# A spectral and token-mixing block, forward and backward on one core: the backward spectral part folded a second time, and its inverse rows interleaved with the weight gradients

## The chip, the core and the metric

One core of a Trainium2 chip. The metric is the device time of one execution, in microseconds; 367.74 us is the median of three runs of the kernel before (366.51 to 368.8). Engines: PE is TensorE, PEld its weight loads, DVE is VectorE, ACT is ScalarE, POOL is GpSimd, SP is SyncE, which issues most of the loads.

## What is computed

The input x has S = 2048 rows and D = 448 columns, bfloat16; F = 1792. Forward:

```python
h   = x + irfft2(rfft2(layernorm(x)) * (w_r + 1j * w_i))   # over rows and columns, 225 half-spectrum columns
u   = gelu(layernorm(h).T @ w1 + b1)                        # 448 x 1792: mixes the 2048 rows
out = h + (u @ w2 + b2).T
```

Outputs are out and the gradients with respect to x, w_r, w_i, w1, b1, w2 and b2 for a given grad_out (out_0 to out_7 in this order). The gradient of the spectral part is again a two-dimensional transform of a 2048 x 448 array (dh), a product with the conjugated weights, and an inverse transform.

## The kernel before

The rows are kept as 16 tiles (h) of 128 partitions. A two-dimensional transform has four steps, all by matrix multiplication with tables:

- fft_rows: for four tiles at a time, VectorE folds the 448 columns into sums and differences of column d and column 448 - d (even and odd part, 225 and 223 columns; L334 to L336), then four 128-wide matmuls a tile (L342) do a 16-point transform, evacuated into zt or zt2.
- fft_cols: for each r of 0 to 8 and its partner 16 - r, eight matmuls 225 columns wide with the table df (L361 to L375), two by two accumulated, then a copy by ScalarE (gi, L378), a sum and a difference by VectorE (gg, L381), three matmuls with hf (L353 to L355) and a copy (L356).
- cmul: the product with the spectral weights on VectorE, in six groups of rows r (L396 to L399); then ifft_cols: 256-wide matmuls (L413, L414) whose weights are 128 columns of the product w_b, and VectorE's sums into ab (L432, L434).
- ifft_rows: for each tile, four 225-wide matmuls with the table di (L443, L445), a ScalarE copy eo of 450 columns, and four matmuls with kinv (L449 to L452).

The program runs: forward spectral part; du = grad through w2 (L472); GELU; out (L627); dh (L683: 14 matmuls 449 columns wide a tile, whose last column is the row's sum of the bias gradient and gives the mean, then norm_back); the backward spectral part; weight gradients gw2 (14 blocks) and gw1 (16 blocks) by outer (L206, L213), each block 16 matmuls and four PSUM banks, copied out by ev (L225 on ScalarE, L226 on VectorE) and stored by POOL. norm_back is ScalarE's v (L650 or L652), then VectorE's L655, L657 and L658. grad_w, the gradient of w_r and w_i, is another cmul, of ds with xs_b, which is loaded again into the slot that goT held.

The order of instructions on each engine is fixed when the program is built: a list scheduler takes ready instructions in the order of the text, by its own estimate of times, and puts later ones that are ready into a wait. issue_after ties one instruction behind another on its engine. Every engine's queue then runs in that order. Tiles come from rings: ps_mm and ps_sp are four PSUM banks each; e4, k1, f2 and w4 have 3, 10, 3 and 4 buffers.

In the text before, the rows of the backward inverse come ahead of gw2 1 to 13, which come ahead of gw1; the scheduler has drawn gw2 and gw1 into the backward spectral part from 235 us on.

Of the kernel before, what the change touches and what calls it, by code (L numbers as in the profile page):

```python
# [11 lines left out]
BF16 = mybir.dt.bfloat16  # L12
# [5 lines left out]
P = 128  # L18
# [23 lines left out]
def _tables():  # L42
# [37 lines left out]
    tb["df1"] = _bf(dtab(wt))  # L80
    tb["df0"] = _bf(dtab(np.ones(DF)))

# [16 lines left out]
    wc[0] = 0  # L99
    tb["di1"] = _bf(itab(wc))  # L100
    pp = np.arange(P)
# [16 lines left out]
def kernel(  # L118
# [211 lines left out]

    def fft_rows(src, zt, g, on, behind=None):
        eo = e4([P, 4, D], "eo")
        a, b = src[:, 4 * g:4 * g + 4, 1:224], src[:, 4 * g:4 * g + 4, 447:224:-1]
        ve.tensor_tensor(out=eo[:, :, 1:224], in0=a, in1=b, op=ALU.add)  # L334
        ve.tensor_tensor(out=eo[:, :, 225:448], in0=a, in1=b, op=ALU.subtract)
        ve.tensor_copy(out=eo[:, :, 0:225:224], in_=src[:, 4 * g:4 * g + 4, 0:225:224])  # L336
        for i in range(4):
            h = 4 * g + i
            pz = ps_sp([P, 4, P])
            with tc.issue_after(behind.ins) if behind is not None else nullcontext():  # L340
                for c, o in enumerate((0, 97, 225, 320)):
                    last = pe.matmul(pz[:, c, :], lhsT=eo[:, i, o:o + P], rhs=kf[:], start=True, stop=True)  # L342
# [3 lines left out]
    def fft_cols(zt, dtab, dst, second=None):  # L346
        e_t = dtab[:, 0:2 * DF].rearrange("p (c k) -> p c k", c=2)
        o_t = dtab[:, 2 * DF:6 * DF].rearrange("p (c s k) -> p c s k", c=2, s=2)

        def out_r(r, gg):  # L350
            px = ps_sp([P, 2 * DF])
            k, i = R_ORDER.index(r) // 8, R_ORDER.index(r) % 8
            pe.matmul(px[:, :], lhsT=hf[:, k, 0, i, :], rhs=gg[:, :], start=True, stop=False)  # L353
            pe.matmul(px[:, 0:DF], lhsT=hf[:, k, 1, i, :], rhs=gg[:, DF:2 * DF], start=False, stop=False)
            pe.matmul(px[:, DF:2 * DF], lhsT=hf[:, k, 2, i, :], rhs=gg[:, 0:DF], start=False, stop=True)  # L355
            ac.copy(out=dst[:, :, r * DF:(r + 1) * DF], in_=px[:, :].rearrange("p (c k) -> p c k", c=2))  # L356

        for r in (0, 8, 1, 2, 3, 4, 5, 6, 7):
            pr = ps_sp([P, 2 * DF])
            for c in range(2):  # L360
                pe.matmul(pr[:, 0:DF], lhsT=zt[:, c, r, :], rhs=e_t[:, c, :], start=(c == 0), stop=(c == 1))  # L361
            for c in range(2):
                pe.matmul(pr[:, DF:2 * DF], lhsT=zt[:, 2 + c, r, :], rhs=o_t[:, c, 0, :],
                          start=(c == 0), stop=(c == 1))
            if r in (0, 8):
                gg = k1([P, 2 * DF], "gg")
                ac.copy(out=gg[:], in_=pr[:])
                out_r(r, gg)
                continue
            pi = ps_sp([P, 2 * DF])  # L370
            for c in range(2):
                pe.matmul(pi[:, 0:DF], lhsT=zt[:, 2 + c, 16 - r, :], rhs=o_t[:, c, 1, :],
                          start=(c == 0), stop=(c == 1))
            for c in range(2):
                pe.matmul(pi[:, DF:2 * DF], lhsT=zt[:, c, 16 - r, :], rhs=e_t[:, c, :],  # L375
                          start=(c == 0), stop=(c == 1))
            gi = f2([P, 2 * DF], "gi")
            ac.copy(out=gi[:], in_=pi[:])  # L378
            for rr, op in ((r, ALU.add), (16 - r, ALU.subtract)):
                gg = k1([P, 2 * DF], "gg")  # L380
                last = ve.tensor_tensor(out=gg[:], in0=pr[:], in1=gi[:], op=op)  # L381
                out_r(rr, gg)
            if r == 2 and second is not None:
                second(last)
# [3 lines left out]

    def cmul(out, a, b, conj, done=None):
        for r0, r1 in R_GROUPS:  # L390
            n = (r1 - r0) * DF
# [12 lines left out]

    def ifft_cols(ys, ab):
        lasts = []

        def half(r):
            pt = ps_sp([P, 2, 2, P])
            lo = 1 if r <= 8 else 0  # L410
            for c in range(2):
                k = r * DF + 97 * c
                pe.matmul(pt[:, c, :, :], lhsT=ys[:, 0, k:k + P], rhs=hi[:, lo:lo + 2, r, :], start=True, stop=False)  # L413
                last = pe.matmul(pt[:, c, :, :], lhsT=ys[:, 1, k:k + P], rhs=hi[:, 1 - lo:3 - lo, r, :],  # L414
                                 start=False, stop=True)
            lasts.append(last)
            return pt
# [19 lines left out]

    def ifft_rows(ab, itab, h):
        a_t = itab[:, 0:2 * DF].rearrange("p (c k) -> p c k", c=2)
# [4 lines left out]
        for c in range(2):  # L444
            pe.matmul(pq[:, DF:], lhsT=ab[:, 1, c, h, :, :], rhs=b_t[:, c, :], start=(c == 0), stop=(c == 1))  # L445
        eo = k1([P, 2 * DF], "eo2")
        ev(eo[:], pq[:], "a")
        py = ps_sp([P, D])
        pe.matmul(py[:, 0:DF], lhsT=kinv[:, 0, :], rhs=eo[:, 0:DF], start=True, stop=False)  # L449
# [63 lines left out]
    for h in range(NT):  # L513
        py = ifft_rows(ab, di0, h)
# [90 lines left out]
    keep(du_d, du, NFB - 2, NFB)  # L605
    ve.tensor_copy(out=du[:, :, D], in_=gb1[:])

# [35 lines left out]
    def norm_back(ps, mean, xhat, rstd_c, back, base, out):  # L643

        v = f2([P, D], "v")
        if mean:
            nm1 = col(1, "nm1")
            ve.tensor_scalar(out=nm1[:], in0=ps[:, D:D + 1], scalar1=rstd_c, scalar2=-1.0 / D,  # L648
                             op0=ALU.mult, op1=ALU.mult)
            ac.activation(out=v[:], in_=ps[:, 0:D], func=ACT.Identity, scale=rstd_c, bias=nm1[:])  # L650
# [12 lines left out]
    di1 = consts.tile([P, 4 * DF], BF16, tag="di", name="di1")  # L663
    w_b = slot(6, [P, 2, XW], "w_b")
    zt2 = slot(2, [P, 4, NR, P], "zt2")
    for h in range(NT):

        if h in (10, 14):
            fft_rows(dh, zt2, h // 4 - 2, "aava", w1_last)
        if h == 4:  # L670
# [3 lines left out]
        if h == 4:  # L674
            with tc.issue_after(w1T_last.ins):
                ld(df0[:], hnd["df0"].ap())
                ld(di1[:], hnd["di1"].ap())
        w1T = w4([P, NFB, P], "w1T")
# [7 lines left out]

    with tc.issue_after(w1T_last.ins):
        load_w(w_b, lambda load, out, in_: load(out, in_))
    fft_rows(dh, zt2, 2, "aava")
# [17 lines left out]
    gw2(0, "aaaa")  # L707
    fft_rows(dh, zt2, 3, "aava", first[0])
    ds = slot(3, [P, 2, XW], "ds")
    fft_cols(zt2, df0, ds)  # L710
# [3 lines left out]
    for h in range(NT):  # L714
        if h % 4 == 0:
            xr = e4([P, 4, D], "xr")
            ld(xr[:], xln_d[:, h:h + 4, :], po)
        py = ifft_rows(ab2, di1, h)
        gx = k1([P, D], "gx")
        norm_back(py, False, xr[:, h % 4, :], rstd_x[:, h:h + 1], -1.0 / D, dh[:, h, :], gx[:])  # L720
        st(rows(out_1[0])[:, h, :], gx[:])


# [11 lines left out]

    for j in range(1, NFB):
        gw2(j, "aaaa" if j < 8 else "aaav")


# [6 lines left out]
    xs_b = slot(4, [P, 2, XW], "xs_b")  # L746


    def grad_w():
        ld(xs_b[:], xs_d[:])  # L750
        o2 = out_2.rearrange("(q r) k -> q (r k)", r=NR)
        o3 = out_3.rearrange("(q r) k -> q (r k)", r=NR)

        def out(r0, r1):
            return xs_b[:, 0, r0 * DF:r1 * DF], xs_b[:, 1, r0 * DF:r1 * DF]

        def done(r0, r1, last):
            st(o2[:, r0 * DF:r1 * DF], xs_b[:, 0, r0 * DF:r1 * DF])
            st(o3[:, r0 * DF:r1 * DF], xs_b[:, 1, r0 * DF:r1 * DF])

        cmul(out, ds, xs_b, True, done)

# [60 lines left out]
```

## Time and profile before

| | |
|---|---|
| runs | 368.8, 367.74, 366.51 us |
| profiled execution | 367.85 us, span 366.1 us |
| TensorE's granted clock | 0.998 |
| HBM read and written | 32.81 and 30.76 MB |
| dh's matmuls end, last group's fold ends | about 228, 234.1 us |
| backward columns and their inverse on TensorE | 236.4 to 275 us |
| inverse rows on TensorE | 276 to 335.9 us |
| last eight gw1 blocks | to 361.4 us |

A line of groups gives line, engine, operation, output and input by name, shapes, count, then total busy time in us and the mean of one in ns, then idle time of the engine just before them and what ended it. The rows of tenths cut the span into 40 equal slices. A matmul's duration holds its way through the array, in which others run too.

### The profile page before, as it was taken

Reading aid. Unit: us, or ns where it says so; the run is one execution under the profiler, and the core shown is the slowest. Engines: PE = TensorE matmul, PEld = TensorE weight load, DVE = VectorE, ACT = ScalarE, POOL = GpSimd, SP = SyncE. Lnnn points to the kernel's source line nnn. Section 1 sums busy time; section 2 is a strip of 40 time slices with the busy share of each in tenths; the row PEclk is TensorE's granted clock in tenths of the full one; section 3 lists DMA queues with packets and bytes.
Section 4 is the critical chain, followed back from the end, with each engine's and each line's share of the span. In section 5 each row is a group of like instructions: output and inputs, shape, how many; then the busy total and the mean of one; then the engine's idle time right before and its main releaser. Section 6 shows DMA issues by size and latency. Waiting matters only on the chain. (4 is left out here: it accounts for less than half of the span.)

```text
span 366.1 us, 5758 instructions
## 1 busy us (share of the span) xinstructions
PE 343.1 (94%) x2115; PEld 190.9 (52%) x2115; DVE 232.3 (63%) x550; ACT 210.7 (58%) x415; POOL 58.0 (16%) x105
## 2 busy tenths in 40 slices
PE   0899998999999999999999999899999999999994
PEld 0556665676655555555554556355664455544442
DVE  4882779887746999522157778637995555699200
ACT  3474553447649997005612243787767666767573
POOL 1000000001122112400340000100121232337310
PEclk9999999999999999999999999999999999999999
DMA  8999999999799999999999879592598356848634
GB/s 284 254 228 337 235 291 259 298 236 312 230 320 181 311 327 215 376 329 308 216 262 237 175 147 280 116 233 88 145 218 259 140 192 231 306 166 288 228 139 163
DMA packets 132989, 87.47 MB, mean 239 GB/s; under 512 B 92033, under 2 KB 123905, under 8 KB 132577
## 3 DMA queue, kind: packets, MB, share of 16 engines
q1 hardware_dynamic: 124768, 56.77, 66.8%
q0 software_dynamic: 8048, 30.31, 22.6%
q8 instruction: 16, 0.26, 0.3%
q14 instruction: 13, 0.10, 0.1%
q10 hardware_dynamic: 144, 0.03, 0.0%
HBM read 32.81 MB, written 30.76 MB: 174 GB/s over the span
## 5 line engine op out<-in xcount | busy, mean ns | idle before, releaser
L225 ACT CAST s<-ps_mm 128x512 bf16<-128x512 f32 x98 | 50.8, 571 | 27.7 <-PE ps_mm L213 18.0
L472 PE MATMUL ps_mm<-go_nat,w2T 128*128 128x448 bf16 x224 | 51.2, 362 | 1.4 <-DMA w2T<-in_B_w_dram 1.4
L683 PE MATMUL ps_mm<-du,w1T 128*128 128x449 bf16 x224 | 43.6, 353 | 0.3 <-DMA w1T<-in_B_w_dram 0.3
L206 PE MATMUL ps_mm<-goT,g_t 128*128 128x512 bf16 x168 | 41.8, 379 | 0.0
L176 POOL DMA_DIRECT2D out_dram<-s x29 | 15.6, 539 | 118.3 <-ACT s L225 102.7
L683 PEld LDWEIGHTS <-w1T 128*128 128x128 bf16 x224 | 21.7, 97 | 21.3 <-DMA w1T<-in_B_w_dram 0.8
L650 ACT ACTIVATE v<-ps_mm,nm,rstd_h 128x448 f32<-128x448 f32 x16 | 11.6, 725 | 36.7 <-DVE nm L648 36.7
L627 PEld LDWEIGHTS <-w2c 128*128 128x128 bf16 x224 | 21.9, 98 | 20.5
L559 PEld LDWEIGHTS <-w1c 128*128 128x128 bf16 x224 | 21.8, 98 | 19.9 <-issue 1.0
L472 PEld LDWEIGHTS <-w2T 128*128 128x128 bf16 x224 | 21.9, 100 | 17.6 <-DMA w2T<-in_B_w_dram 2.7
L206 PE MATMUL ps_mm<-du_t,hlnT 128*128 128x512 bf16 (+1 forms) x144 | 30.4, 353 | 0.0
L627 PE MATMUL ps_mm<-gT,w2c 128*128 128x448 bf16 x112 | 30.3, 352 | 0.0
L627 PE MATMUL ps_sp<-gT,w2c 128*128 128x448 bf16 x112 | 30.3, 352 | 0.0
L206 PEld LDWEIGHTS <-hlnT 128*128 128x128 bf16 x192 | 17.9, 98 | 19.8 <-issue 4.6
L381 DVE TENSOR_TENSOR gg<-ps_sp,gi 128x450 bf16<-128x450 f32 x28 | 16.2, 621 | 18.0 <-ACT gi L378 17.9
L559 PE MATMUL ps_mm<-hln,w1c 128*128 128x448 bf16 x112 | 23.8, 352 | 0.3 <-ACT hln L327 0.3
L206 PEld LDWEIGHTS <-g_t 128*128 128x128 bf16 x168 | 16.1, 97 | 14.0 <-issue 1.1
L559 PE MATMUL ps_sp<-hln,w1c 128*128 128x448 bf16 x112 | 22.8, 352 | 0.0
L225 ACT CAST eo<-ps_sp 128x450 bf16<-128x450 f32 x32 | 17.2, 538 | 9.5 <-PE ps_sp L445 9.2
L655 DVE CUSTOM_DVE_ANT_0 junk<-v,xr 128x448 bf16<-128x448 f32 x16 | 10.0, 624 | 19.8 <-ACT v L652 19.8
L639 ACT ACTIVATE junk<-go_r 128x448 bf16<-128x448 bf16 x16 | 9.2, 576 | 22.7 <-DMA go_r<-in_grad_out_dram 22.2
L632 DVE SCALAR_TENSOR_TENSOR h<-ps_mm,b2col,hr 128x448 bf16<-128x448 f32 x8 | 5.1, 679 | 25.8 <-PE ps_mm L627 25.8
(151 smaller groups left out, 653.1 us busy)
## 6 DMA issues: line engine op xcount, KB each, us to landing
w1c<-in_B_w_dram SPq DMA_DIRECT2D x7, 1024.0 KB, 8.7
w2c<-in_B_w_dram SPq DMA_DIRECT2D x8, 896.0 KB, 13.6
out_dram<-s POOLq DMA_DIRECT2D x14, 512.0 KB, 4.1
out_dram<-s POOLq DMA_DIRECT2D x15, 448.0 KB, 2.9
xs_d<-xs SPq DMA_DIRECT2D x1, 1800.0 KB, 7.6
xs_b<-xs_d SPq DMA_DIRECT2D x1, 1800.0 KB, 8.1
x<-in_A_x_dram SPq DMA_DIRECT2D x4, 448.0 KB, 4.4
go_nat<-in_grad_out_dram SPq DMA_DIRECT2D x2, 896.0 KB, 7.1
```

Source lines behind the costliest of these rows:

```text
L176: return (eng or po).dma_start(out=out, in_=in_)
L206: last = pe.matmul(ps, lhsT=lhs[:, c, a], rhs=rhs[:, c, b], start=opens and c == 0, stop=not opens and c == 2)
L225: return ac.copy(out=out, in_=in_)
L381: last = ve.tensor_tensor(out=gg[:], in0=pr[:], in1=gi[:], op=op)
L472: pe.matmul(pg[:], lhsT=w2T[j][:, t, :], rhs=go_nat[:, t, :], start=(t == 0), stop=(t == NT - 1))
L559: pe.matmul(pu[:], lhsT=wc[:, h, o:o + P], rhs=hln[:, h, :], start=(h == 0), stop=(h == NT - 1))
L627: pe.matmul(p2[i][:], lhsT=w2c[t0 // 4][:, j, i * P:(i + 1) * P], rhs=gT[:, j, :], start=(j == 0), stop=(j == NFB - 1))
L632: ve.scalar_tensor_tensor(out=h2[:], in0=p2[i][:], scalar=b2col[:, t:t + 1], in1=hr[:, i, :], op0=ALU.add, op1=ALU.add)
L639: ac.activation(out=junk[:], in_=go_r[:, h, :], func=ACT.Copy, accum_out=gb2[:, h:h + 1])
L650: ac.activation(out=v[:], in_=ps[:, 0:D], func=ACT.Identity, scale=rstd_c, bias=nm1[:])
L655: ve.tensor_tensor_reduce(out=junk[:], in0=v[:], in1=xhat, scale=back, scalar=0.0, op0=ALU.mult, op1=ALU.add, accum_out=nm2[:])
L683: w1_last = pe.matmul(pd[:], lhsT=w1T[:, j, :], rhs=du[:, j, 0:D + 1], start=(j == 0), stop=(j == NFB - 1))
```

## The change

The backward transform alone (twice=True) folds its columns a second time: fold_2 makes sums and differences of column d and 224 - d of the even and the odd part. Even and odd frequencies then each need one 113-column matmul per part in place of two accumulated 225-column ones; sums and by_k put the frequencies back in order as VectorE writes. The inverse does the same backwards: ifft_cols takes every other column of w_b as weights, and rows_mid_twice makes four 113-column matmuls, a ScalarE copy (od) of half of them and two VectorE sums in place of a ScalarE copy of the whole. Table contents change with it.

The inverse rows' first step is issued two tiles ahead. gw2 1 to 5 come ahead of the rows in the text; one gw2 block (6 to 13) stands behind each of tiles 0 to 7, one gw1 block (0 to 7) behind each of tiles 8 to 15, and one group of grad_w behind each of tiles 10 to 15. VectorE copies a bank of eight gw2 blocks, formerly of six. xr has a ring of its own. The mean column of dh is scaled by -1/D in du, so that ScalarE alone takes it from PSUM. g_t's doubling copy and goT's come ahead of the loads of w_b.

```diff
-    def fft_rows(src, zt, g, on, behind=None):
+    def fold_2(eo, src, g):
+        e2 = e4([P, 4, 2 * DF], "e2")
+        v = eo[:].rearrange("p i (a d) -> p i a d", a=2)
+        a, b = v[:, :, :, 1:113], v[:, :, :, 223:111:-1]
+        ve.tensor_tensor(out=e2[:].rearrange("p i (a d) -> p i a d", a=2)[:, :, :, 1:113], in0=a, in1=b, op=ALU.add)
+        ve.tensor_tensor(out=e2[:, :, 2:450].rearrange("p i (a d) -> p i a d", a=2)[:, :, :, 112:224],
+                         in0=a, in1=b, op=ALU.subtract)
+        for o, op in ((0, ALU.add), (113, ALU.subtract)):
+            ve.tensor_tensor(out=e2[:, :, o:o + 1], in0=src[:, 4 * g:4 * g + 4, 0:1],
+                             in1=src[:, 4 * g:4 * g + 4, 224:225], op=op)
+        return e2
+    def fft_rows(src, zt, g, on, behind=None, twice=False):
         eo = e4([P, 4, D], "eo")
...
-        ve.tensor_copy(out=eo[:, :, 0:225:224], in_=src[:, 4 * g:4 * g + 4, 0:225:224])
+        if twice:
+            eo = fold_2(eo, src, g)
+        else:
+            ve.tensor_copy(out=eo[:, :, 0:225:224], in_=src[:, 4 * g:4 * g + 4, 0:225:224])
...
-                for c, o in enumerate((0, 97, 225, 320)):
+                for c, o in enumerate((0, 113, 226, 322) if twice else (0, 97, 225, 320)):
                     last = pe.matmul(pz[:, c, :], lhsT=eo[:, i, o:o + P], rhs=kf[:], start=True, stop=True)
...
+        def part(out, r, odd, s=0):
+            if twice:
+                for c, chunk in enumerate((3, 2) if odd else (0, 1)):
+                    o = 113 * ((2 + 2 * s if odd else 0) + c)
+                    pe.matmul(out[:, 113 * c:113 * c + 113], lhsT=zt[:, chunk, r, :], rhs=dtab[:, o:o + 113],
+                              start=True, stop=True)
+                return
+            for c in range(2):
+                o = DF * (2 + 2 * c + s if odd else c)
+                pe.matmul(out, lhsT=zt[:, 2 * odd + c, r, :], rhs=dtab[:, o:o + DF], start=(c == 0), stop=(c == 1))
...
+        def sums(nm):
+            gg = k1([P, 2, w], nm)
+            return gg, gg[:].rearrange("p a (k c) -> p a c k", c=2) if twice else gg[:]
+        def by_k(ps):
+            return ps[:].rearrange("p a (c k) -> p a c k", c=2) if twice else ps[:]
...
+            pr = ps_sp([P, 2, w])
+            part(pr[:, 0, :], r, 0)
+            part(pr[:, 1, :], r, 1, 0)
...
+                gg, out = sums("gg")
+                last = ve.tensor_tensor(out=out, in0=by_k(pr), in1=by_k(gi), op=op)
...
+                k = r * DF + (c if twice else 97 * c)
+                ks = slice(k, k + 2 * P - 1, 2) if twice else slice(k, k + P)
+                pe.matmul(pt[:, c, :, :], lhsT=ys[:, 0, ks], rhs=hi[:, lo:lo + 2, r, :], start=True, stop=False)
+                last = pe.matmul(pt[:, c, :, :], lhsT=ys[:, 1, ks], rhs=hi[:, 1 - lo:3 - lo, r, :],
...
+    def rows_mid_twice(ab, itab, h):
+        pq = ps_sp([P, 2, 2, 113])
+        for i, (kind, c) in enumerate(((0, 0), (0, 1), (1, 1), (1, 0))):
+            last = pe.matmul(pq[:, i // 2, i % 2, :], lhsT=ab[:, kind, c, h, :, :],
+                             rhs=itab[:, 113 * i:113 * i + 113], start=True, stop=True)
+        eo = k1([P, 2 * DF], "eo2")
+        out = eo[:].rearrange("p (a d) -> p a d", a=2)
+        od = f2([P, 2, 113], "od")
+        ac.copy(out=od[:], in_=pq[:, :, 1, :])
+        ve.tensor_tensor(out=out[:, :, 0:113], in0=pq[:, :, 0, :], in1=od[:], op=ALU.add)
+        ve.tensor_tensor(out=out[:, :, 224:112:-1], in0=pq[:, :, 0, 0:112], in1=od[:, :, 0:112], op=ALU.subtract)
+        return eo, last
...
+    ve.tensor_scalar(out=du[:, :, D], in0=gb1[:], scalar1=-1.0 / D, scalar2=None, op0=ALU.mult)
...
-            ve.tensor_scalar(out=nm1[:], in0=ps[:, D:D + 1], scalar1=rstd_c, scalar2=-1.0 / D,
-                             op0=ALU.mult, op1=ALU.mult)
+            ac.activation(out=nm1[:], in_=ps[:, D:D + 1], func=ACT.Copy, scale=rstd_c)
...
+    w_b = slot(6, [P, 2, XW + 32], "w_b")
+    po.memset(w_b[:, :, XW:XW + 32], 0.0)
...
+            fft_rows(dh, zt2, h // 4 - 2, "aava", w1_last, True)
...
-    with tc.issue_after(w1T_last.ins):
-        load_w(w_b, lambda load, out, in_: load(out, in_))
...
     ld_t4(g_t[:], gT_d[:])
+    ld_twice(g_t, w1T_last)
     ld_twice(goT, w1T_last)
-    ld_twice(g_t, w1T_last)
+    with tc.issue_after(w1T_last.ins):
+        load_w(w_b[:, :, 0:XW], lambda load, out, in_: load(out, in_))
+    fft_rows(dh, zt2, 2, "aava", None, True)
...
+    fft_rows(dh, zt2, 3, "aava", first[0], True)
...
+    fft_cols(zt2, df0, ds, None, True)
...
     ab2 = slot(7, [P, 2, 2, NT, NR, 8], "ab2")
-    ifft_cols(w_b, ab2)
...
-    for j in range(1, NFB):
-        gw2(j, "aaaa" if j < 8 else "aaav")
...
-    for h in range(8):
+    def gw1_four(h):
         outs, out = gw1(h, ps_mm)
         outer(outs[:2], outs[2:], hlnT, du_t)
         out()
-        if h == 3:
-            grad_w()
...
+        cmul(out, ds, xs_b, True, done, (group,))
...
+    for j in range(1, 6):
+        gw2(j, "aaaa")
+    mids = [rows_mid_twice(ab2, di1, h) for h in range(2)]
+    for h in range(NT):
+        if h + 2 < NT:
+            mids.append(rows_mid_twice(ab2, di1, h + 2))
+        if h % 4 == 0:
+            xr = ring.tile([P, 4, D], BF16, tag="xr", bufs=2, name="xr")
+            ld(xr[:], xln_d[:, h:h + 4, :], po)
+        with tc.issue_after(mids[-1][1].ins):
+            py = rows_out(mids[h][0])
+        gx = k1([P, D], "gx")
+        norm_back(py, False, xr[:, h % 4, :], rstd_x[:, h:h + 1], -1.0 / D, dh[:, h, :], gx[:])
+        st(rows(out_1[0])[:, h, :], gx[:])
+        if h < 8:
+            gw2(h + 6, "aaav")
+        else:
+            gw1_four(h - 8)
+        if h == 7:
+            ld(xs_b[:], xs_d[:])
+        if h > 9:
+            grad_w(R_GROUPS[h - 10])
```

More of the change, by code (lines that the diff above doesn't have):

```diff
@@ L350, in out_r @@
         def out_r(r, gg):
-            px = ps_sp([P, 2 * DF])
+            px = ps_sp([P, 2, DF])
             k, i = R_ORDER.index(r) // 8, R_ORDER.index(r) % 8
[L353 to L356, printed above, removed]
+            pe.matmul(px[:, :, :], lhsT=hf[:, k, 0, i, :], rhs=gg[:, :, 0:DF], start=True, stop=False)
@@ L358, in fft_cols @@
+            pe.matmul(px[:, 0, :], lhsT=hf[:, k, 1, i, :], rhs=gg[:, 1, 0:DF], start=False, stop=False)
+            pe.matmul(px[:, 1, :], lhsT=hf[:, k, 2, i, :], rhs=gg[:, 0, 0:DF], start=False, stop=True)
+            ac.copy(out=dst[:, :, r * DF:(r + 1) * DF], in_=px[:])
         for r in (0, 8, 1, 2, 3, 4, 5, 6, 7):
-            pr = ps_sp([P, 2 * DF])
-            for c in range(2):
-                pe.matmul(pr[:, 0:DF], lhsT=zt[:, c, r, :], rhs=e_t[:, c, :], start=(c == 0), stop=(c == 1))
@@ L362, in fft_cols @@
-            for c in range(2):
-                pe.matmul(pr[:, DF:2 * DF], lhsT=zt[:, 2 + c, r, :], rhs=o_t[:, c, 0, :],
-                          start=(c == 0), stop=(c == 1))
+            pr = ps_sp([P, 2, w])
+            part(pr[:, 0, :], r, 0)
+            part(pr[:, 1, :], r, 1, 0)
             if r in (0, 8):
-                gg = k1([P, 2 * DF], "gg")
-                ac.copy(out=gg[:], in_=pr[:])
+                gg, out = sums("gg")
+                ac.copy(out=out, in_=by_k(pr))
                 out_r(r, gg)
@@ L369, in fft_cols @@
                 continue
[L370 to L377, printed above, removed]
+            pi = ps_sp([P, 2, w])
+            part(pi[:, 0, :], 16 - r, 1, 1)
@@ L387, with cmul @@
     R_GROUPS = ((0, 3), (14, 16), (3, 6), (11, 14), (6, 8), (8, 11))
-    def cmul(out, a, b, conj, done=None):
-        for r0, r1 in R_GROUPS:
+    def cmul(out, a, b, conj, done=None, groups=R_GROUPS):
+        for r0, r1 in groups:
             n = (r1 - r0) * DF
```

80 lines of the change are left out of this document (40 added, 40 removed).

## The prediction

> **What bounds the kernel now.** I read the page first: which engine is full, and where.
>
> ```profile
> PE 343.1 (94%) x2115; PEld 190.9 (52%) x2115; DVE 232.3 (63%) x550; ACT 210.7 (58%) x415; POOL 58.0 (16%) x105
> PE   0899998999999999999999999899999999999994
> DVE  4882779887746999522157778637995555699200
> PEclk9999999999999999999999999999999999999999
> ```
>
> TensorE is full from end to end at full clock, so a microsecond of matmul removed is a microsecond gained, unless an order of waits gives it back. The changed part runs from 226 us (end of dh) to 361 us (last matmul); the 4.7 us behind it, ScalarE's last copies and the last stores, are not touched. Next, the groups of instructions from 190 us on, shapes kept apart (line, engine, operation, shapes, count, busy us and mean ns, idle before).
>
> ```profile
> L443 PE MATMUL ps_sp<-di,ab 128*128 128x225 bf16 x32 | 5.7, 261 | 0.0
> L445 PE MATMUL ps_sp<-di,ab 128*128 128x225 bf16 x32 | 5.8, 260 | 0.0
> L361 PE MATMUL ps_sp<-df,zt 128*128 128x225 bf16 x18 | 3.2, 261 | 0.0
> L372 PE MATMUL ps_sp<-df,zt 128*128 128x225 bf16 x14 | 2.5, 260 | 0.0
> L342 PE MATMUL ps_sp<-kf,eo 128*128 128x128 bf16 x64 | 4.2, 219 | 1.3 <-DVE eo L336 1.3
> L225 ACT CAST eo<-ps_sp 128x450 bf16<-128x450 f32 x16 | 8.7, 546 | 0.0
> L381 DVE TENSOR_TENSOR gg<-ps_sp,gi 128x450 bf16<-128x450 f32 x14 | 8.1, 621 | 9.6 <-ACT gi L378 9.5
> L432 DVE TENSOR_TENSOR ab<-ps_sp,t 128x512 bf16<-128x512 f32 x7 | 4.8, 688 | 0.0
> L648 DVE TENSOR_SCALAR nm<-ps_mm,rstd_h 128x1 f32<-128x1 f32 x14 | 2.9, 211 | 0.0
> L334 DVE TENSOR_TENSOR eo<-go_r 128x892 bf16<-128x892 bf16 x4 | 2.5, 626 | 0.1
> ```
>
> The reader is to see the 225-wide matmuls, 128 in all (L361, L363, L372, L375: 18+18+14+14; L443, L445: 32+32). A duration of 260 ns is not what one costs, since matmuls overlap. The cost is the distance of starts, read from the timeline:
>
> ```profile
> 227.89 1.05 PE L342 MATMUL ps_sp<-kf,eo 128*128 128x128 bf16 x16
> 232.45 0.39 DVE L658 TENSOR_TENSOR go_r<-junk,go_r 128x448 bf16<-128x448 bf16 x1
> 234.19 1.07 PE L342 MATMUL ps_sp<-kf,eo 128*128 128x128 bf16 x16 [1.34 <-DVE eo L336]
> 243.20 0.36 PE L361 MATMUL ps_sp<-df,zt 128*128 128x225 bf16 x2
> 243.40 0.36 PE L363 MATMUL ps_sp<-df,zt 128*128 128x225 bf16 x2
> ```
>
> Two 225-wide ones take 0.20 us (median start to start 96.5 ns); sixteen 128-wide ones, each with its own weights, take (1.05 - 0.22)/15 = 55.5 ns each. With 108.6 ns at 256 columns and 215.6 at 512, that is a line of 0.417 ns a column plus 2.2 ns. Last, what TensorE waits for from 190 us on:
>
> ```profile
> PE ps_sp L342 <- DVE eo L336: 1.3, 1, 1.3
> PE ps_sp L449 <- ACT eo L225: 1.3, 4, 0.4
> PE ps_sp L353 <- DVE gg L381: 0.7, 2, 0.4
> PE ps_mm L213 <- DMA g_t<-g_t: 0.4, 1, 0.4
> ```
>
> This view counts only time in which no matmul was in flight. By starts, against the line above, TensorE loses 9.3 us between 226 and 361 us: 1.9 around the last backward group (eo 1.5, g_t 0.4), 2.6 ahead of L353, 3.1 ahead of L449, 0.7 in the inverse columns, and 1.0 in crumbs. The other 125.7 us are streaming.
>
> **The change, part by part.**
>
> Matmul width. 128 matmuls go from 225 to 113 columns, the count stays. By the line 113 columns are 49.3 ns: 128 x (96.5 - 49.3) = 6.0 us less. If the pace stops at the narrowest row (55.5 ns), 5.2 us. I take 6.0, since 128-wide ones still lie on the line. In a sentence apart: the Trainium skill, TensorE: Matmul & The Clock Gate, section Back-to-back issue gap, gives about 81 ns for each 128-wide matmul in a stream with weight loads; the 55.5 ns of L342, which are such a stream, do not agree, and by that figure the term would be 128 x (96.5 - 81) = 2.0 us.
>
> Stepped weights. The inverse columns load every other element of w_b as weights (64 loads under 256-wide matmuls). No row has stepped weights. A load takes 98 ns here and hides under 108.6 ns; the bounds are nothing and a second load's length left bare, 64 x 98 ns = 6.3 us. I take nothing, as all load rows, whole or 64 rows high, are 94 to 100 ns. The Trainium skill, same page, section Weight-path perf modes, says that the fast load also takes stepped columns; no run shows it yet.
>
> dh's mean. VectorE loses 16 of L648 (0.21 us) and ScalarE gains 16 one-column operations, about 0.2 us each by L648. What counts is the order: now VectorE comes to tile 15's L648 only behind tile 14's norm (at 229.99, though the matmuls ended near 228), and finishes dh at 232.84. Afterwards ScalarE can start at 228.1: 0.2 + 0.7 (L650), then VectorE's chain of 1.8 (tile 14: 228.29 to 230.07): 230.9. The second fold then costs two more 0.54 us steps (L334's pace; 896 elements for 892) and two small ones in place of one, 1.3 + 1.3 = 2.6: eo at 233.5, against 234.13. The first three groups' folds, 1.3 us each, lie under dh's 2.7 us of matmul per tile, where VectorE gains slack by the loss of L648. ScalarE's three zt copies (0.55 each) may push tile 15 back by half a microsecond, and the list may put a gw2 piece into the wait. So -0.4 us, bounds -1.9 and +0.6. g_t's doubling copy moves ahead of w_b's 1.8 MB on SP's queue: it lands sooner, w_b some 1.5 us later (around 232, first read at 246.6); hidden.
>
> Forward columns of the block (L353's wait). Same chain: ScalarE gi, VectorE two sums (452 for 450, a stepped write, one element a cycle as PSUM already makes it), TensorE. TensorE's own share shrinks by 0.19 us for every four matmuls, so more filler is wanted: now 97 matmuls of gw2, six blocks, are spread from 235 to 277. gw2 1 to 5 stand first in the text and 6 on have no dependence on the rows, so the list can still draw on them. The stepped slices of w_b also reach 31 columns into the next row, so that row 2 waits for cmul's third group and row 5 for its fifth; their last writes (L399) start at 259.84 and 265.86, and those weights are loaded no earlier than 263.5 and 269.8: hidden. Taken as unchanged, bounds -1 and +2.
>
> Inverse rows. ScalarE's eo copy (450, 546 ns) becomes a copy of 226 (some 350, on the slope of 546 at 450 and 372 at 256 columns), and VectorE adds two sums: by 688 at 512 and 621 at 450, 226 columns are 380 ns, 0.30 to 0.35 start to start, so 0.6 to 0.76 a tile; if width did not count, 1.24. The first step is two tiles, some 7 us, ahead of its use, so the 3.1 us ahead of L449 go. xr leaves the e4 ring, which POOL waited for (7.3 us in three waits), so its four loads and the gx stores behind them only come sooner. xs_b's load on SP's queue has nothing behind it but the last four stores; the memset of w_b's padding waits on POOL for the last read of w2c, behind the out_0 stores, 50 us ahead of need. No time for these. Two of gw2's banks move from ScalarE to VectorE (0.68 each), hidden.
>
> What is late next: VectorE. A tile with gw2 is 0.58 + 3.25 = 3.8 us of matmul against 1.80 + 0.7 + 0.68 = 3.2 on VectorE: enough. Tiles 10 to 15 carry a gw1 block (2.8 + 0.58 = 3.4 us) and a grad_w group (2.45 us for three, 1.75 for two): 4.5 to 4.9 us on VectorE. It falls back 1.3 us a tile; tile 15's sums stand behind three groups, 3.9 us late, plus some 1 to 2 for xs_b, which may load only after gw2 13 and took 8.1 us to land, two tiles being 6.8. The lead of 6.8 us about covers it, and behind the rows lie eight gw1 blocks (22 us) that VectorE is not in. I charge 0.8 us, bounds 0 and 3.
>
> Sum against the profiled execution (367.85 us; span 366.1 and 1.75 around it; the median of the runs is 0.1 lower): -6.0 - 0.4 - 3.1 + 0.8 = -8.7, so 359.2 us.
>
> **Rivals.**
> 1. The rows give most back: waits of 0.2 to 0.5 us a tile as before, now on VectorE, 16 x 0.3 = 4.8 us. For it: 4.9 against 3.4 us in six tiles. Against: the two tiles' lead. 364.
> 2. Weight loads pace the narrow matmuls: every one brings 128 new columns, a load takes 98 ns (its row beside L443), and if no two overlap, the pace stays where it is and the 6.0 us are not gained: 365.2. Against: the sixteen of L342, 55.5 ns apart, each with a load of 98 ns. By the 81 ns of the Trainium skill above it would be 363.2.
> 3. Stepped weights are loaded slower than the matmul above them hides: +6.3: 365.5.
> 4. Slower. VectorE's queue is in order, and in tiles 10 to 15 sums for tile h+2 stand behind a grad_w group. If the lead is used up when tile 10 begins (xs_b late, VectorE behind from the gw2 tiles), TensorE, whose second step is tied behind tile h+2's first, walks at VectorE's pace: at the far bound of 1.24 for the sums 5.5 us against 3.4, 6 x 2.1 = 12.6: 367.85 - 9.5 + 12.6 = 371. It decides from the point at which VectorE's lag passes 6.8 us before tile 13; my values give 4 to 6. For it: VectorE already has no gap from 322 to 340 us. Against: VectorE is 63% busy overall, and TensorE has 22 us of work that needs none of it, which the list may draw forward.
>
> **Numbers.** Forecast 0.62; rivals 1: 0.13, 2: 0.05, 3: 0.06, 4: 0.14. The forecast's own range is 357 to 362 (all waits gone; or the pace at 55.5 with the row bounds). Leaving out 2 in 10, on the slow side mostly, gives 356.5 to 365.5. Faster by over 1% (under 364.1; 1% is about what this kernel's measurement can tell from none) are the forecast and half of rival 1: 0.685; within 1% half of rival 1 and rivals 2 and 3: 0.175; slower 0.14.
>
> **What would show it.** 113-wide matmuls about 49 ns apart; TensorE's busy time some 6 us lower; no wait of L353's kind growing; no wait of the rows' second step on its sums; eo of the last group near 233.5 us; the rows' two sums each under 0.4 us. Wrong if TensorE waits on VectorE in tiles 10 to 15, if weight loads in the inverse columns spread the 256-wide matmuls beyond 108.6 ns, or if gaps open between 235 and 277 us because the filler ran out.

## The result, and the profile after

| | us |
|---|---|
| before, median of 6 runs | 367.88 (366.51 to 368.8) |
| after, median of 6 runs | 360.8 (360.18 to 362.35) |
| ratio, after to before | 0.9829, 95% interval 0.9807 to 0.9851 |
| profiled run of after (span) | 361.35 (359.5) |

So 1.7% less: 7.1 us by the medians, 6.5 by the two profiled runs. The forecast was 359.2, 1.6 us too low. Ratios, here and below, leave out executions more than 1.5% above the fastest of the same kernel (two of e9's, one of e14's); medians do not.

The page of after, with the engines' busy time, then TensorE and VectorE over 40 slices:

```profile
PE 334.7 (93%) x2100; PEld 184.9 (51%) x2115; DVE 243.9 (68%) x580; ACT 210.5 (59%) x429; POOL 58.1 (16%) x106
PE   0799996999999999999999999989999999999994
DVE  4883776967773999822226887837799997599600
```

Two places stand out. TensorE's seventh slice (54 to 63 us) has gone from 8 to 6: that is in the forward part, which the diff was not about. And VectorE's slices 31 to 33 (270 to 297 us), the start of the inverse rows, have gone from 5 to 9, with TensorE at 9 above them: VectorE took on the sums and TensorE kept going. (15 matmuls have no record in this trace, 2100 of 2115; all are in the weight-gradient blocks.)

The groups of after from 190 us on, shapes apart, as before:

```profile
L488 PE MATMUL ps_sp<-di,ab 128*128 128x113 bf16 x64 | 5.9, 214 | 0.0
L388 PE MATMUL ps_sp<-df,zt 128*128 128x113 bf16 x64 | 4.8, 213 | 0.2 <-ACT zt L243 0.2
L376 PE MATMUL ps_sp<-kf,e 128*128 128x128 bf16 x64 | 4.2, 219 | 0.2 <-DVE e L355 0.2
L493 ACT COPY od<-ps_sp 128x226 f32<-128x226 f32 x16 | 5.5, 359 | 3.3 <-PE ps_sp L488 1.5 <-DVE junk L720 1.2 <-ACT s L243 0.5
L494 DVE TENSOR_TENSOR eo<-ps_sp,od 128x226 bf16<-128x226 f32 x16 | 6.2, 388 | 2.5 <-ACT od L493 2.5
L495 DVE TENSOR_TENSOR eo<-ps_sp,od 128x224 bf16<-128x224 f32 x16 | 6.1, 381 | 0.0
L426 DVE TENSOR_TENSOR gg<-ps_sp,gi 128x452 bf16<-128x452 f32 x14 | 8.5, 664 | 8.3 <-ACT gi L423 8.3
L354 DVE TENSOR_TENSOR e<-eo 128x896 bf16<-128x896 bf16 x4 | 2.5, 628 | 0.0
```

All 128 narrow matmuls stand in L488 and L388. The rows' copy and two sums cost 359, 388 and 381 ns, where 350 and 380 were estimated. The new work is no dearer than forecast; what it does to TensorE is in the timeline and the waits.

The timeline of after at the end of dh:

```profile
229.93 1.05 PE L376 MATMUL ps_sp<-kf,e 128*128 128x128 bf16 x16
232.78 0.39 DVE L721 TENSOR_TENSOR go_r<-junk,go_r 128x448 bf16<-128x448 bf16 x1
235.79 1.07 PE L376 MATMUL ps_sp<-kf,e 128*128 128x128 bf16 x16 [0.23 <-DVE e L355]
241.52 0.58 PE L388 MATMUL ps_sp<-df,zt 128*128 128x113 bf16 x8
```

dh itself ends at 229.74 us for 227.69: **everything ahead of the changed part is 2.05 us later.** After that the last norm ends 3.43 us behind the last dh matmul (before: 5.15), and the wait for the last group is 0.23 us for 1.34.

What TensorE waits for in after from 190 us on:

```profile
PE ps_sp L405 <- DVE gg L426: 1.0, 4, 0.4
PE ps_sp L405 <- ACT gg L416: 0.5, 1, 0.5
PE ps_mm L224 <- issue: 0.5, 3, 0.2
PE ps_sp L376 <- DVE e L355: 0.2, 1, 0.2
```

No line for L512, the rows' second step, remains. Made into a ledger by starts (each matmul at 0.417 ns a column plus 2.2 ns, a pair on two halves of the array as one, 95 ns where the height of the weights changes; the rest is a wait of the one that follows; unrecorded matmuls added), from the last dh matmul to the last matmul of all:

| us | before | after | difference |
|---|---|---|---|
| the changed part | 133.44 | 124.80 | -8.65 |
| of it streaming | 124.13 | 118.56 | -5.57 |
| waits, ahead of rows' second step (L449, L512) | 3.22 | 0.20 | -3.02 |
| waits, ahead of hf matmuls (L353, L405) | 2.63 | 2.91 | +0.28 |
| waits, ahead of row transforms (L342, L376) | 1.52 | 0.42 | -1.10 |
| other waits | 1.95 | 2.71 | +0.76 |
| all ahead of it, start to last dh matmul | 227.69 | 229.74 | +2.05 |

Two of the unrecorded matmuls, 0.43 us, stand just ahead of hf matmuls and are not counted as waits there: the trace of e9 below has the same order, the same T and all 2115 records, and shows them.

The changed part gained almost exactly what was forecast (8.7). Two microseconds were lost where nothing was looked for. The waits over the whole run name the place, first before, then after:

```profile
PE ps_mm L472 <- DMA w2T<-in_B_w_dram: 1.4, 2, 1.1
```

```profile
PE ps_mm L535 <- DMA w2T<-in_B_w_dram: 4.1, 2, 3.5
```

L535 is the dg stage, whose weights w2T come by transposing loads. Its last matmul starts at 92.03 us before and 94.55 after. The queues of that time (SPq is SP's own DMA queue, in order; POOL issues its own; a row's time is that of issuing, and the data land later), before:

```profile
47.70 8.16 SPq L179 DMA_TRANSPOSE w2T<-in_B_w_dram  x2
56.04 2.94 SPq L173 DMA_DIRECT2D w1c<-in_B_w_dram  x2
59.02 7.03 SPq L179 DMA_TRANSPOSE w2T<-in_B_w_dram  x1
```

and after, SP's and POOL's:

```profile
47.45 10.71 SPq L197 DMA_TRANSPOSE w2T<-in_B_w_dram  x2
58.33 2.27 SPq L191 DMA_DIRECT2D w1c<-in_B_w_dram  x2
60.65 8.26 SPq L197 DMA_TRANSPOSE w2T<-in_B_w_dram  x1
...
50.73 0.57 POOL L191 DMA_DIRECT2D xr<-xln_d  x1 [48.27 <-DMA xln_d<-xln]
51.81 0.55 POOL L191 DMA_DIRECT2D xr<-xln_d  x1 [0.50 <-DMA xln_d<-xln]
```

With a ring of its own xr waits for no buffer, only for xln_d, whose stores are issued up to 45.6 us; its first two loads (448 KB each) start at 50.7 and 51.8 us, 216 us earlier than before (266.8, 269.4). They are in flight beside the pair in the first row, the ninth and tenth loads of w2T. The ninth lands at 58.69 us, 11.2 behind the start of its issue (before: at 56.46, 8.8 behind). Issuing the tenth takes 4.5 us, from 53.6 on (before: 2.0, from 53.9), and all that is behind it on SP's queue comes later. The ninth block of dg, which reads the ninth load, starts at 58.7 for 56.5.

### The profile page after: what moved, and what is told of

Same layout as the page of the kernel before. It is cut to its first block, busy times and chain, and to the rows that moved or that the text cites. A ratio compares the mean times of both kernels' runs of the same rounds, so it can differ in the third digit from the quotient of the medians.

```text
span 359.5 us, 5818 instructions
## 1 busy us (share of the span) xinstructions
PE 334.7 (93%) x2100; PEld 184.9 (51%) x2115; DVE 243.9 (68%) x580; ACT 210.5 (59%) x429; POOL 58.1 (16%) x106
## 4 chain that ended last, share of the span: by engine, by line
PE 71%; DVE 12%; ACT 7%; DMA 7%; issue 2%; ACTq 0%; DVEq 0%
PE ps_mm L224 13%; PE ps_mm L748 12%; PE ps_mm L622 6%; PE ps_sp L691 6%; PE ps_mm L691 6%; DMA w2T<-in_B_w_dram 6%; PE ps_mm L535 6%; PE ps_sp L622 5%; PE ps_mm L231 3%; PE ps_sp L224 2%; ACT s L243 2%; DVE bs_x L324 1%; PE ps_sp L405 1%; ACT zt L243 1%; PE ps_sp L376 1%
## 5 line engine op out<-in xcount | busy, mean ns | idle before, releaser
L243 ACT CAST s<-ps_mm 128x512 bf16<-128x512 f32 x96 | 48.4, 568 | 20.1 <-PE ps_mm L231 13.1
L535 PE MATMUL ps_mm<-go_nat,w2T 128*128 128x448 bf16 x224 | 50.9, 361 | 4.1 <-DMA w2T<-in_B_w_dram 4.1
L535 PEld LDWEIGHTS <-w2T 128*128 128x128 bf16 x224 | 21.8, 99 | 20.0 <-DMA w2T<-in_B_w_dram 5.4
L426 DVE TENSOR_TENSOR gg<-ps_sp,gi 128x450 bf16<-128x450 f32 (+1 forms) x28 | 16.6, 642 | 16.8 <-ACT gi L423 16.8
L712 ACT ACTIVATE nm<-ps_mm,rstd_h 128x1 f32<-128x1 f32 x16 | 4.2, 262 | 33.8 <-PE ps_mm L748 33.8
L224 PEld LDWEIGHTS <-g_t 128*128 128x128 bf16 x168 | 15.1, 97 | 15.5 <-issue 3.9
L243 ACT CAST zt<-ps_sp 128x512 bf16<-128x512 f32 x26 | 13.4, 596 | 6.9 <-PE ps_sp L376 6.9
L578 DVE TENSOR_TENSOR x<-ps_sp,x 128x448 bf16<-128x448 f32 x16 | 10.0, 625 | 9.5 <-PE ps_sp L515 8.6
```

Source lines behind the costliest of these rows:

```text
L224: last = pe.matmul(ps, lhsT=lhs[:, c, a], rhs=rhs[:, c, b], start=opens and c == 0, stop=not opens and c == 2)
L243: return ac.copy(out=out, in_=in_)
L426: last = ve.tensor_tensor(out=out, in0=by_k(pr), in1=by_k(gi), op=op)
L535: pe.matmul(pg[:], lhsT=w2T[j][:, t, :], rhs=go_nat[:, t, :], start=(t == 0), stop=(t == NT - 1))
```

## The experiments

**The theory.** (a) Fold and order need each other: the fold frees streaming time, the order and the two tiles' lead keep it from coming back as waits in the rows. (b) The 2 us lost ahead of dh are xr's early loads, beside a transposing load. Rivals: to (a), that one half alone brings the gain, or that VectorE's new sums are the limit; to (b), that the forward part merely scatters.

"T" below is the changed part of the ledger, from a trace; "total" is the median of timed runs, beside the ratio to before. The last column is the time of issuing w2T's tenth load.

| run | total, us | ratio to before (95%) | T, us | issue of w2T's tenth load, us |
|---|---|---|---|---|
| e1_fold_only | 367.53 | 1.0013 (0.9987 to 1.004) | 134.44 | 2.0 |
| e2_order_only | 368.24 | 1.0038 (1.0011 to 1.0064) | 130.01 | 4.5 |
| e3_no_lead | 369.93 | 1.0083 (1.0053 to 1.0113) | 132.73 | 4.5 |
| e4_mean_on_vector | 364.16 | 0.992 (0.9889 to 0.995) | 126.59 | 4.5 |
| e5_sums_twice | 363.18 | 0.9908 (0.9881 to 0.9934) | 125.76 | 4.5 |
| e6_text_order | 364.81 | 0.9938 (0.9912 to 0.9964) | 126.40 | 4.5 |
| e9_xr_late | 363.01 | 0.986 (0.9816 to 0.9904) | 124.80 | 2.0 |
| e10_before_xr_ring | 369.49 | 1.0081 (1.0049 to 1.0112) | 131.62 | 4.5 |
| a2_changed_again | 362.01 | 0.9825 (0.978 to 0.9871) | 124.80 | 4.5 |
| e13_xr_behind_gw2 | 359.59 | 0.9763 (0.9717 to 0.9809) | 124.80 | 2.0 |
| e14_cols_lead | 357.95 | 0.97 (0.9656 to 0.9744) | 122.91 | 2.0 |
| e15_forward_fold | 366.79 | 0.9968 (0.9937 to 1.0) | 124.80 | 2.2 |

**The fold alone** (the functions and tables of after; order, lead, mean and xr's ring of before).

> The kernel before plus the second fold alone: no lead in the inverse rows, gw2, gw1 and grad_w where they stood in the text, the mean column on VectorE, the loads in their old order. Theory (the fold is worth its streaming, the order is worth the waits): 6.0 us of streaming go, but the inverse rows' chain gets longer (ScalarE 0.36 and two VectorE sums of 0.3 and 0.38 in place of one copy of 0.55), so the waits ahead of the second step grow from 3.1 us to some 8 us: about 367 us, hardly faster than before. Rival (fillers take every wait): about 362 us, the whole 6.0 us.

As expected: no gain at all. Streaming fell to 118.3 us, as in after, and the waits rose from 9.3 to 16.1: 5.9 of them ahead of the rows' second step, 4.6 ahead of weight-gradient blocks. Some 1.6 us of the 4.6 is no wait: from 318.86 us on, behind a wait of 2.0 us in the rows, the granted clock is 0.5 for 3.41 us, and 512-wide matmuls start some 427 ns apart, for 216. (The trace is of the longest of its ten executions.) From the waits of its whole run:

```profile
PE ps_sp L512 <- DVE eo L495: 3.0, 5, 2.0
```

**The order alone** (order, lead and loads of after with the single fold and its tables; the mean on VectorE).

> The changed kernel with single-fold tables, matmuls and steps of before, the mean on VectorE and the old loads: what is left of the change is the order (first step two tiles ahead, a gw2 or gw1 block behind each tile, grad_w by groups, xr's own ring). Theory: the 3.1 us ahead of the rows' second step go and nothing else: about 364.8 us, TensorE's streaming as before. Rival (the list scheduler interleaved already, the order is worth nothing): 367.9 us.

The changed part did what was expected, T 3.4 us shorter, rows' waits 0.14 us. The total did not: 368.24, not the 364.8 expected. That miss is what led to (b), since this kernel too has xr's ring, and shows the same 4.5 us for the tenth load's issue and the same wait:

```profile
PE ps_mm L535 <- DMA w2T<-in_B_w_dram: 3.3, 1, 3.3
```

Fold alone +1.0 us of T, order alone -3.4, the whole change -8.65: 6.25 us are in neither. Not all of that comes from fold and order together. The mean on ScalarE, which both runs leave out, is 1.8 of it (e4 below), and e1's stretch at half clock some 1.6. By these traces about 2.8 us are left to the pair, with the new order of the loads, which no run separates.

**After without the lead.**

```diff
-    mids = [rows_mid_twice(ab2, di1, h) for h in range(2)]
+    mids = []
...
-        if h + 2 < NT:
-            mids.append(rows_mid_twice(ab2, di1, h + 2))
+        mids.append(rows_mid_twice(ab2, di1, h))
```

> The changed kernel with the rows' first step issued in its own tile, not two tiles ahead. Theory: each tile's second step waits for ScalarE's copy and two VectorE sums, 0.5 us or more a tile that the list underestimates: 16 x 0.5 = 8 us, about 368 us. Rival (the block behind each tile is drawn into the wait): at most 1 us, about 361.5 us.

T is 7.9 us longer than after's, the total 1.0083 of before's where after has 0.9829 (9.3 us), and the wait is the one named:

```profile
PE ps_sp L512 <- DVE eo L495: 4.2, 13, 0.6
```

Thirteen of 16 tiles wait for the second sum, 0.6 us at most. This is what the lead is worth, and it is more than before's 3.2 us of such waits: with the fold, the rows' path is a copy and two sums, where it was one copy.

**dh's mean back on VectorE.**

```diff
-            ac.activation(out=nm1[:], in_=ps[:, D:D + 1], func=ACT.Copy, scale=rstd_c)
+            ve.tensor_scalar(out=nm1[:], in0=ps[:, D:D + 1], scalar1=rstd_c, scalar2=None, op0=ALU.mult)
```

> The changed kernel with dh's mean column taken by VectorE again (same numbers, other engine). Theory: the last tile's norm ends some 1.9 us later, but gw2 1 covers it: 0 to 0.5 us slower, 361 us. Rival (the start of the backward columns is the path): 1.5 to 2 us slower, 362.5 us.

T is 1.8 us longer, all of it between the last dh matmul and the first column matmul (9.89 us for 8.11; 116.70 and 116.69 behind it). The norm ends 5.23 us behind the last dh matmul, for 3.43. The experiment's rival was right, and the prediction's -0.4 for this start was a net of two terms: the mean saves 1.8, the second fold costs 1.3 of it again. Two of the waits show who stands in the queue:

```profile
PE ps_sp L376 <- DVE e L355: 0.7, 1, 0.7
...
PE ps_mm L231 <- ACT v L713: 0.4, 1, 0.4
```

The second is a matmul of a gw2 block, waiting for a bank of ps_mm that tile 15's v frees, and v waits for VectorE's mean.

**The sums made twice,** to load VectorE in the rows.

```diff
-        ve.tensor_tensor(out=out[:, :, 0:113], in0=pq[:, :, 0, :], in1=od[:], op=ALU.add)
-        ve.tensor_tensor(out=out[:, :, 224:112:-1], in0=pq[:, :, 0, 0:112], in1=od[:, :, 0:112], op=ALU.subtract)
+        for _ in range(2):
+            ve.tensor_tensor(out=out[:, :, 0:113], in0=pq[:, :, 0, :], in1=od[:], op=ALU.add)
+            ve.tensor_tensor(out=out[:, :, 224:112:-1], in0=pq[:, :, 0, 0:112], in1=od[:, :, 0:112], op=ALU.subtract)
```

> The changed kernel with VectorE's two sums of each inverse row written twice: the same values, 0.65 us more on VectorE in each of 16 tiles (10 us in all). Theory (VectorE's lag stays inside the two tiles' lead and the 22 us of gw1 behind the rows): at most 1 us slower, 361 to 362 us. Rival (VectorE sets the pace in tiles 10 to 15, the fourth rival of the prediction): 4 us or more slower, 365 us.

T rose by 1.0 us for 32 more sums, 12.3 us of work on VectorE. The prediction's fourth rival, TensorE at VectorE's pace, is out. The windows of after show why (columns: stretch, its length, busy time of PE, PEld, DVE, ACT, POOL, then the granted clock, DMA share, GB/s):

```profile
316.00:321.00 5.00, 4.95 (x33) 2.21 (x31) 5.00 (x15) 3.21 (x9) 2.15 (x4) 1.00 0.31 117
321.00:326.00 5.00, 5.00 (x37) 2.81 (x36) 5.00 (x12) 3.65 (x10) 1.70 (x4) 1.00 0.42 155
326.00:331.00 5.00, 4.84 (x31) 2.17 (x29) 5.00 (x13) 3.69 (x9) 3.11 (x6) 1.00 0.82 302
331.00:336.00 5.00, 5.00 (x33) 2.33 (x30) 5.00 (x12) 2.87 (x7) 3.00 (x6) 1.00 0.58 205
```

VectorE is busy 5.00 of 5.00 us and TensorE 4.84 to 5.00: the list drew matmuls that need no VectorE between the tiles, so the rows end at 329.18 us, and 25.35 us of matmul still follow them.

**The blocks behind the rows again in the text** (lead kept).

```diff
-    for j in range(1, 6):
-        gw2(j, "aaaa")
...
-        if h < 8:
-            gw2(h + 6, "aaav")
-        else:
-            gw1_four(h - 8)
...
+    for j in range(1, NFB):
+        gw2(j, "aaaa" if j < 8 else "aaav")
+    for h in range(8):
+        gw1_four(h)
...
```

> The changed kernel with the lead of two tiles kept, but gw2 1 to 13 and then gw1 0 to 7 behind all rows in the text, grad_w whole behind gw1 3, as before. Theory (the list scheduler interleaves them by itself; the lead is what counts): within 1 us of the changed kernel, 361 us. Rival (the fixed blocks are what removes the waits): 3 us slower, 364 us.

T is 1.6 us longer, between the theory and the rival; the median is beyond the rival's 364. The rows ran through without filler, done at 314.3 us, and the waits went to their first step, which finds its bank held:

```profile
PE ps_sp L488 <- ACT v L715: 1.6, 5, 0.4
```

So of the order it is the lead that counts most: without it T loses 7.9 us (e3), without the fixed blocks 1.6.

In e4, e5 and e6 the medians stand 3.4, 2.4 and 4.0 us above after's, more than T explains (1.8, 1.0, 1.6). The rest lies ahead of T and was not separated; their traces have a stretch at half clock near 60 us, shown for e10 below, which after's trace has not.

**xr tied behind the forward's last out store.**

```diff
-            ld(xr[:], xln_d[:, h:h + 4, :], po)
+            with tc.issue_after(h2_last.ins):
+                ld(xr[:], xln_d[:, h:h + 4, :], po)
```

> The changed kernel with xr's loads tied on POOL's queue behind the last store of out (about 200 us), nothing else. Theory (the two xr loads that the own ring lets go at 50.7 us delay the tenth transposing load of w2T from 2.0 to 4.5 us, and TensorE waits 3.5 us for it): that load is back at 2 us, dg ends some 2.2 us earlier, about 358.6 us. Rival (the forward loads differ from run to run for other reasons): 360.8 us, dg's end as in the changed kernel.

The first half came as expected: 2.0 us for the tenth load's issue, dg's last matmul at 92.19. But the loads, now at 188.6 and 189.1 us, met the next transposing loads, those of w1T, and dh, which reads w1T, took 52.4 us for 44.5. The tile's summary in after, then in e9 (min, median and max of one issue in ns), and e9's wait:

```profile
L197 SPq DMA_TRANSPOSE w1T<-in_B_w_dram x16: 1461/1585/8034, 106.0 to 218.5; - x16
```

```profile
L197 SPq DMA_TRANSPOSE w1T<-in_B_w_dram x16: 1461/1734/9125, 103.6 to 224.0; - x16
...
PE ps_mm L748 <- DMA w1T<-in_B_w_dram: 4.6, 1, 4.6
```

The issue of 9.1 us is the one that began at 191.5, beside xr; in its place, third in a row, the other traces have 1.5 to 2.1. From 200.32 us on, 1 us ahead of the end of the wait of 4.6 us, the granted clock is 0.5 for 6.83 us: an estimated 2.9 us more, and the two make up most of dh's delay. But this trace is of one of the two longest executions (366.89 and 373.13); the other four took 358.94 to 363.26, and whether they had this wait is not known. The total is unclear for that reason.

**Before with xr's ring, and nothing else.**

```diff
-            xr = e4([P, 4, D], "xr")
+            xr = ring.tile([P, 4, D], BF16, tag="xr", bufs=2, name="xr")
```

> The kernel before with one edit: xr from a ring of its own with two buffers, as in the changed kernel. Theory: the same two loads start near 50 us, the tenth w2T load takes 4.5 us, some 2 us slower, 369.5 us; the inverse rows unchanged. Rival: no difference, 367.4 us.

This isolates it. One line makes the kernel before slower by 0.8% (interval 0.5 to 1.1), though T gets 1.8 us shorter (so part of what e2 gained in T can be the ring's too). Its queues and its wait (both views of this kernel):

```profile
48.27 10.46 SPq L179 DMA_TRANSPOSE w2T<-in_B_w_dram  x2
...
51.32 0.58 POOL L173 DMA_DIRECT2D xr<-xln_d  x1 [48.85 <-DMA xln_d<-xln]
52.39 0.55 POOL L173 DMA_DIRECT2D xr<-xln_d  x1 [0.49 <-DMA xln_d<-xln]
```

```profile
PE ps_mm L472 <- DMA w2T<-in_B_w_dram: 3.9, 2, 3.6
```

Over all traces of the study, with before and after among them: in the eight with xr at 49.8 to 53.1 us, the tenth load's issue takes 4.5 us and the ninth load lands 10.7 to 11.9 us behind the start of its issue; in the six with xr later it is 2.0 to 2.2 and 8.1 to 9.7. The wait on w2T by itself separates them less well, since other loads of that tile scatter too (e1, without early xr, waited 4.3 us, in three pieces of 1.6 at most).

A second cost stands behind this wait, and after's trace does not have it. The same 3 us in e10, then in after:

```profile
60.30:63.30 3.00, 3.00 (x12) 1.60 (x11) 2.46 (x5) 1.05 (x2) 0.00 (x0) 0.50 0.89 245
60.30:63.30 3.00, 3.00 (x26) 2.32 (x24) 3.00 (x6) 1.57 (x3) 0.00 (x0) 1.00 1.02 289
```

In e10 the granted clock is 0.50, and 12 matmuls stand there for 26. Seven of the eight traces with early xr, all but after's, are at 0.5 for 3.41 us beginning between 58.6 and 60.3 us, from 0.4 us ahead to 1.2 us behind the end of waits of 2.6 to 3.7 us; the ninth block of dg starts 8.9 to 9.2 us ahead of the tenth there, and 7.5 in after and in before. No trace with xr later has this near 60 us. By 3.41 us at half clock that is an estimated 1.7 us on top of the wait at most. Why after's wait of 3.5 us was not followed by it, these traces do not show.

**After with xr behind gw2 3,** in a stretch in which no transposing load is issued; the changed kernel again beside it.

```diff
-    for j in range(1, 6):
-        gw2(j, "aaaa")
+    kept = [gw2(j, "aaaa") for j in range(1, 6)]
...
-            ld(xr[:], xln_d[:, h:h + 4, :], po)
+            with tc.issue_after(kept[2].ins):
+                ld(xr[:], xln_d[:, h:h + 4, :], po)
```

> The changed kernel as it is, for a comparison on the same chip as the next runs: 360.8 us; the two xr loads near 50 us and a tenth w2T load of 4.5 us again; from dh's last matmul to the last matmul 124.8 us.

> The changed kernel with xr's loads tied on POOL's queue behind the store of gw2 3, past the last transposing load of w1T. Theory (the loads cost only where they meet transposing loads on which TensorE waits): the tenth w2T load is 2.0 us, dh takes 44.5 us again, and the gain of the changed part stays: 2 us under the changed kernel, 358.6 us. Rival (the forward differs by chance): the same as the changed kernel.

The loads start at 250.7 and 251.2 us, T stays at 124.80, and the wait returns to where it was before the change:

```profile
PE ps_mm L535 <- DMA w2T<-in_B_w_dram: 1.2, 3, 0.6
```

2.4 us less than the changed kernel by the medians on the same chip (359.59 for 362.01; 358.6 was expected). Their intervals against before overlap, so for the size e10's is the firmer test; the sign is the same in both.

**e13, with the hf matmuls of the backward columns held behind the next pair's narrow ones,** to give VectorE's sums time.

```diff
+        def flush(after):
+            while late:
+                with tc.issue_after(after.ins):
+                    out_r(*late.pop(0))
...
-                out_r(r, gg)
+                late.append((r, gg))
```

> The kernel of the run before, with the backward columns' three hf matmuls (L405 to L407) held back until the next pair of rows r has had its 113-wide matmuls, so that they no longer wait for VectorE's sums. Theory (the waits ahead of L405, 3.3 us by starts in the changed kernel, are the list's underestimate of ScalarE and VectorE, and a lead takes them as it did in the rows): 2 to 3 us under the run before, 356 us. Rival (the chain through VectorE is the path there, the wait moves to the inverse columns): no gain.

T 1.9 us shorter: the waits ahead of the hf matmuls fall from 3.35 to 1.01 us, those ahead of the narrow matmuls and the inverse columns rise by 1.3 and 0.7, 0.6 is less streaming (the ledger counts fewer changes of the weights' height), and the other 0.9 is fewer waits elsewhere. Both traces lack 15 matmuls, so a single row can be off by some 0.4. 357.95 us, 3.0% below before (interval 2.6 to 3.4), the best of the versions, and 1.6 below e13 where 2 to 3 were expected.

**e13, with the forward block folded twice as well** (lead of two tiles there too).

> The kernel of xr behind gw2, with the forward transform folded twice as well and its inverse rows' first step two tiles ahead: another 128 matmuls from 225 to 113 columns. Theory (TensorE's streaming is what counts): 5 to 6 us under it, 353 us. Rival (the forward part waits for w2T's loads and for VectorE, which gets some 15 us more work there; busy matmul time is no bound): no gain or some us slower.

128 more matmuls are narrower, and it is 7.2 us slower than e13. T is unchanged; the out stage starts 7.5 us later (146.91 for 139.38). Its waits in the forward part:

```profile
PE ps_sp L379 <- DVE e L358: 13.0, 3, 12.4
PE ps_mm L538 <- DMA w2T<-in_B_w_dram: 4.7, 3, 2.3
PE ps_mm L630 <- ACT hln L348: 1.9, 2, 1.3
PE ps_sp L379 <- DVE nb_x L340: 1.5, 1, 1.5
```

The first line, 10.9 us in after, is the wait for the input's first fold. Twice, from 71.69 and from 105.82 us, the granted clock is also at 0.5 for 3.41 us, an estimated 1.7 us each; e13 has no such stretch. The rival was right: in this part, where TensorE waits for others, the fold gained nothing.

## Why the prediction held, step by step

- **What bounds it:** right for the changed part (T -8.65 for -8.7 forecast), wrong for the whole. TensorE's 94% hid that dg runs close behind its loads: before waits 1.4 us on w2T, 1.1 of it at 56 us, and the prediction, which listed waits from 190 us on, never weighed that line. (Its stretch from 226 us also holds dh's last 1.7 us, which changes nothing in its sum.)
- **The step that failed:** "xr leaves the e4 ring, which POOL waited for (7.3 us in three waits), so its four loads and the gx stores behind them only come sooner", and behind it "No time for these." Sooner was taken for harmless; it was 216 us sooner and beside a transposing load. Size: +2.05 us up to the end of dh in the profiled run of after; between 2.4 us (e13 against the changed kernel) and 4.8 (e10: +3.0 in total where T fell by 1.8). The stretch at half clock fits the upper figure: seven of e10's eight executions have a mean clock of 0.993 to 0.995 over the span, as its trace has, and only three of the changed kernel's twelve are at 0.993. Any of these sizes covers the 1.6 us between forecast and median.
- **Width:** 113-wide matmuls start 52.3 ns apart on average, for 49.3 by the line and 55.5 as the bound: 128 x (96.5 - 52.3) = 5.7 us for 6.0. Both groups (L488, L388) have starts 49 to 55 ns apart, with means of 52.4 and 52.2; no cause was sought. Rival 2 is out. The 81 ns that the Trainium skill (TensorE: Matmul & The Clock Gate, Back-to-back issue gap) gives for 128-wide matmuls in such a stream do not agree with these, nor with the 56 ns of the 128-wide ones at L376.
- **Stepped weights:** nothing, as taken. The 256-wide matmuls over them start 108 to 109 ns apart, with loads of 98 ns. Rival 3 is out. By the Trainium skill, same page, Weight-path perf modes, the fast load takes stepped columns too; the trace agrees in that these loads take no longer than the others.
- **dh's mean and the second fold:** norm 1.7 us sooner for 1.9; the second fold 2.56 us for 2.6; the start of the columns -0.63 for -0.4.
- **Forward columns of the block:** taken as unchanged, bounds -1 and +2; +0.3 ahead of the hf matmuls. e14 takes more than that from these waits.
- **Rows:** -3.0 for -3.1. Rival 1 is out, by the waits.
- **VectorE late in tiles 10 to 15:** 0 for +0.8. The lag was as feared, since VectorE sat 3.23 us for xs_b's load at tile 10 and then ran without a gap to 336 us; the lead and the unbound blocks took all of it. Rival 4 is out.

By the rows of the ledger the misses inside the changed part are +0.4 (streaming, for width), +0.1 (rows), +0.3 (hf matmuls) and -0.7 (row transforms, 1.1 for 0.4). The 0.8 charged to VectorE did not come, but other waits, which the prediction did not name, grew by nearly the same. So it cancels: that the sum came out to 0.05 us is luck, the terms are right to within 0.8.

## What to carry to other kernels

A fold that shortens matmuls gained here only where TensorE sets the pace, and only with the order that hides the longer path behind it: alone it brought nothing, and the whole change without the lead 0.7 us of T in place of 8.65. A buffer of its own is also permission to start: ask when the transfer will now begin, and what is on the wires then; if nothing needs it early, tie it to a place where nothing else is loading. And read the waits of the whole run, also where the diff does not reach, with the granted clock behind each: a wait can cost more than its length.

## What the hardware showed that was not expected

A transposing load came later when ordinary loads were in flight from another queue. With two loads of 448 KB issued by POOL near 50 us, w2T's ninth load landed 10.7 to 11.9 us behind the start of its issue, for 8.1 to 9.7, and issuing the tenth took 4.5 us for 2.0 to 2.2 (eight traces against six; e10 has this one edit alone). SP's queue is in order, so all behind it moved with it. One issue of w1T of 9.1 us, for 1.5 to 2.1, beside the same loads (e9) is a single trace. What the loads share, a port, the memory or the transfer engines, these traces do not show.

TensorE's granted clock fell to 0.5 for 3.41 us about the end of waits of 2.6 to 3.7 us (seven traces; 6.83 us about 4.6 in e9), and behind some of 1.3 to 2.0 us (e1, e15), but not behind after's of 3.5. What decides it is open.
